# Two of four block transposes moved from TensorE to the DMA crossbar, beside the opening loads

## The chip, the cores and the metric

One core of one Trainium2 chip. The time is device microseconds of one execution; a kernel is run several times and the median is quoted. The kernel before takes 215.1 us (215.06 to 215.31 in its first three runs).

## The reference

A layer norm feeds a sliding, dilated local attention (32 heads of 20, 8 keys at distance 0, 2, ... 14) and a dense MLP with GELU; both are added to the input.

```python
S, D, F, H, W, dil = 2048, 640, 1536, 32, 8, 2
xn  = layernorm(x)                               # (2048, 640), bf16
qkv = xn @ wqkv                                  # 640 -> 1920
logits[h, s, w] = q[h, s] . k[h, s - 2*w] * 20**-0.5      # masked where s - 2*w < 0
att = softmax(logits) applied to v[h, s - 2*w]
out = x + att @ wo + gelu(xn @ w1 + b1) @ w2 + b2
```

## The kernel before

The 2048 rows are worked in four chunks of 512, a chunk in four blocks of 128 rows. Every matmul over D here takes the normalised rows transposed (`xnT`). In chunks 1 to 3 a DMA does that (`dma_start_transpose` from one SBUF tile to another, called a crossbar transpose below; one of a block with nothing beside it landed 2.4 us after its issue), issued from the SP queue from 20.5 us on, when the opening loads are nearly over. In chunk 0 TensorE does it, five 128x128 transposes a block into PSUM and a copy on ScalarE out of it, since the DMA engines are still busy with loads (94% from 6.5 to 25.3 us). The q, k and v projections of chunk 0 are made block by block, so that work can begin when the first block is there: 75 matmuls of 128x128 a block, in five groups.

A small planner in the kernel (class `Plan`) orders all pieces: each has an engine, an assumed length, needs, PSUM buffers and a rank; the emitted order per engine is then fixed.

```python
nc.sync.dma_start(x_sb[:, 0, :], x_nb[:, 0, :])
nc.scalar.dma_start(x_sb[:, 1, :], x_nb[:, 1, :])
for s in range(3):                                           # wq, wk, wv
    nc.sync.dma_start(wqkv[s][:], wqkv_v[:, :, s * D : (s + 1) * D])
    if s == 0:
        nc.sync.dma_start(x_sb[:, 2:BPC, :], x_nb[:, 2:BPC, :])
...
for n in range(1, NCH):                                      # chunks 1 to 3 of x
    cs = slice(n * BPC, (n + 1) * BPC)
    nc.sync.dma_start(x_sb[:, cs, :], x_nb[:, cs, :])
nc.sync.dma_start(w1_sb[:], ...)                             # first MLP weights
...
def do_tp(n, bl):                                            # chunk 0, TensorE
    tp = psA.tile([P, 2 * CH], BF16, tag="acc", name="tp")
    for t in range(KT):
        nc.tensor.transpose(tp[:, t * P : (t + 1) * P], xn[:, t * P : (t + 1) * P], ident[:])
def do_tc(n, bl):                                            # chunk 0, ScalarE
    nc.scalar.copy(xnT[:, :, bl * P : (bl + 1) * P], tp[:, 0 : KT * P]...)
def do_td(n, bl):                                            # chunks 1 to 3, crossbar
    nc.sync.dma_start_transpose(xnT[:, :, bl * P : (bl + 1) * P], tiles["xn", n, bl][:])
def do_gj(bl, g):                                            # one group of a block's projections
    ...
    for i, (which, to) in enumerate(slots):
        for ti in range(KT):
            nc.tensor.matmul(ps[:, i, :], lhsT=wqkv_p[which][:, ti, to, :],
                             rhs=tiles["xnT", 0][:, ti, cs], start=(ti == 0), stop=(ti == KT - 1))
```

Of the kernel before, what the change touches and what calls it, by code (L numbers as in the profile page):

```python
# [11 lines left out]
ALU = mybir.AluOpType  # L12
AX = mybir.AxisListType
BF16 = mybir.dt.bfloat16
F32 = mybir.dt.float32
PE, VE, SE, DQ = "pe", "ve", "se", "dq"


class Plan:
# [101 lines left out]
S, D, F, H, W, DIL = 2048, 640, 1536, 32, 8, 2  # L121
P = 128
# [3 lines left out]
CH = 512  # L126
# [7 lines left out]
LASTB = S // P - 1  # L134
# [4 lines left out]


RANK = {
    "ad02": 53.9, "ad11": 29.1, "av2": -13.3, "f11": 8.8, "f12": -3.3, "gc1": 31.2, "ge3": -70.6, "gj1": 9.7,
    "gj2": -47.4, "o01": 8.4, "o02": -60.5, "o10": 1.1, "o11": -5.1, "o23": -111.4, "oc1": 83, "pj11": -38.5,
    "pj21": -36.7, "qk3": -41.5, "st2": 58.4, "st3": 210.8, "xn1": 20.2, "xn2": 19.2,
}


def make_plan(fns, offsets=RANK):

    pl = Plan(offsets)  # L150
# [6 lines left out]
    def f(kind, *a):  # L157
        return lambda: fns[kind](*a)
# [6 lines left out]
    for n in range(NCH):  # L165
        base = n * PERIOD
        prev = base - PERIOD
        early = base + (-37.0 if n == 1 else -85.0)
        xnT, q, k, v, oT = (("xnT", n), ("q", n), ("k", n), ("v", n), ("oT", n))
# [11 lines left out]
        for bl in range(BPC):  # L181
            xn, tp = ("xn", n, bl), ("acc", "tp", n, bl)
            pl.add(f"xn{n}{bl}", SE if n else VE, 0.81 if n else 0.42, early + -4.0 if n else -99, [f"rc{n}" if n else f"rc{n}{bl}"], f("xn", n, bl), [xn])
            if n > 0:
                pl.add(f"tc{n}{bl}", DQ, 4.0 if n > 1 else 2.7, early - 3.0, [f"xn{n}{bl}"], f("td", n, bl), [xn, xnT], 21.5)
                continue
            pl.add(f"tp{n}{bl}", PE, 0.3, early + -3.0 if n else -99, [f"xn{n}{bl}"], f("tp", n, bl), [xn, tp])
            pl.add(f"tc{n}{bl}", SE, 0.65, early + -3.0 if n else -99, [f"tp{n}{bl}"], f("tc", n, bl), [tp, xnT])
# [5 lines left out]
        if n == 0:  # L194
            for bl in range(BPC):
                for g, parts in enumerate(GROUPS):
                    ps, last = ("acc", "g", bl, g), max(p[0] for p in parts)
# [57 lines left out]
        for bl in range(BPC):  # L255
            ob = ("osb", n, bl)
            O = [("O", n, bl)] if n < NCH - 1 or bl % 2 == 0 else [("acc", "lo", n, bl), ("acc", "hi", n, bl)]
            final = n * BPC + bl == LASTB
            last = None
            for pc in range(5):  # L260
                need = [last] if last else [f"ge{n}{ft}" for ft in range(FT)] + [f"xb{n}", "ld"]
                if pc == 4:
                    need.append(f"ot{n}")
                us = (0.65, 0.65, 0.65, 0.65, 1.08)[pc] if final else (0.82, 0.82, 0.82, 0.82, 1.37)[pc]
                last = pl.add(f"o{n}{bl}{pc}", PE, us, base + PERIOD + 8.0 + 8.0 * bl, need, f("o", n, bl, pc, ("lo",) if final else ("lo", "hi")), O + (hTs if pc == 0 else hTs[3 * pc : 3 * pc + 3] if pc < 4 else [oT]))
            if final:
                pl.add("xl", VE, 0.42, base - 40, ["ld"], f("xl"))
                pl.add("oclo", VE, 0.65, base, [last, "xl"], f("oclo"), O + [ob])
                last = pl.add("ohi", PE, 1.05, base + PERIOD + 90, [last], f("ohi"), O)
                pl.add("ochi", VE, 0.25, base, [last], f("ochi"), O + [ob])  # L270
                continue
            pl.add(f"oc{n}{bl}", SE, 0.78, base, [last], f("oc", n, bl), O + [ob])
            pl.add(f"od{n}{bl}", SE, 0.0, base, [f"oc{n}{bl}"], f("od", n, bl), [ob])
# [4 lines left out]
def kernel(  # L278
# [16 lines left out]
    nc = tc.nc  # L295
# [6 lines left out]
    consts = ctx.enter_context(tc.tile_pool(name="consts", bufs=1))  # L302
# [15 lines left out]
    x_sb = wts.tile([P, NCH * BPC, D], BF16, name="x_sb")  # L318
# [3 lines left out]
    wo2 = wts.tile([P, KT, D], BF16, name="wo2")  # L322
    b1_rt = consts.tile([P, P], BF16, name="b1_rt")
    b2bc = consts.tile([P, D], BF16, name="b2bc")
    xlast = consts.tile([P, D], BF16, name="xlast")
    wqkv_v = A_wqkv.rearrange("(t p) n -> p t n", p=P)
    b2_bcast = bass.AP(tensor=B_b2.tensor, offset=B_b2.offset, ap=[[0, P], [1, D]])
    nc.sync.dma_start(x_sb[:, 0, :], x_nb[:, 0, :])
# [48 lines left out]
    tiles = {}  # L377

    def get(key, make):
        if key not in tiles:  # L380
            tiles[key] = make()
        return tiles[key]
# [48 lines left out]
    def do_tc(n, bl):  # L431
# [3 lines left out]
            tiles["tp", n, bl][:, 0 : KT * P].rearrange("p (t m) -> p t m", t=KT),  # L435
        )

    def do_td(n, bl):
        xnT = get(("xnT", n), lambda: xtp.tile([P, KT, CH], BF16, tag="xnT", name="xnT"))
        nc.sync.dma_start_transpose(xnT[:, :, bl * P : (bl + 1) * P], tiles["xn", n, bl][:])  # L440
# [12 lines left out]
        nc.gpsimd.dma_start(dst, b2bc[:].unsqueeze(1).to_broadcast([P, cs.stop - cs.start, D]), accum_op=ALU.add)  # L453

    def do_xl():
        nc.vector.tensor_tensor(out=xlast[:], in0=x_sb[:, LASTB, :], in1=b2bc[:], op=ALU.add)


    def qkv_tile(n, which):
# [224 lines left out]
    last = (NCH - 1, BPC - 1)  # L684

    def do_oclo():
        osb = outp.tile([P, D], BF16, tag="osb", name="osb")
        tiles["osb", last] = osb
        nc.vector.tensor_tensor(out=osb[:, 0:CH], in0=tiles["lo", *last][:], in1=xlast[:, 0:CH], op=ALU.add)  # L689
        nc.sync.dma_start(out_sd[LASTB * P :, 0:CH], osb[:, 0:CH])  # L690

    def do_ohi():
# [3 lines left out]
    def do_ochi():  # L696
        osb = tiles["osb", last]
        nc.vector.tensor_tensor(  # L698
            out=osb[:, CH:D], in0=tiles["hi", *last][:, 0 : D - CH], in1=xlast[:, CH:D], op=ALU.add
        )  # L700
        nc.scalar.dma_start(out_sd[LASTB * P :, CH:D], osb[:, CH:D])

# [2 lines left out]
    with tc.manual_schedule(engines=engines):  # L705

        idle = psA.tile([P, CH], F32, tag="acc", name="idle")
        for _ in range(WARM):
            nc.tensor.matmul(idle[:, 0:P], lhsT=ident[:], rhs=ident[:], start=True, stop=True)
        for t in make_plan(fns).run():  # L710
            t["fn"]()
# [30 lines left out]
```

## Time and profile before

| stage of the profiled execution (span 212.9 us) | from, us | to, us |
|---|---|---|
| warm-up matmuls on the identity, first loads | 0 | 6.5 |
| projections of chunk 0 | 6.5 | 25.3 |
| MLP, attention, projections of chunks 1 to 3, output | 25.3 | 210.1 |
| last sum and store | 210.1 | 212.9 |

TensorE has hardly a pause between its first transpose and its last matmul, and the chain that ended last consists of it for 95%. So a change pays by what it takes off TensorE, or costs by the time that TensorE stands still. (The windows leave it 1.8 us idle.) The first MLP matmul starts at 25.32 us; from there to the end it is 187.6 us. I use these two numbers below as "the end of the projections" and "the rest". The lines are shown in the prediction.

### The profile page before, as it was taken

The numbers are of one execution on the slowest core, as the hardware profiler recorded it, in microseconds if no ns is written. First come the engines' busy times: TensorE is split into PE (matmuls) and PEld (weight loads), VectorE is DVE, ScalarE is ACT, GpSimd is POOL, SyncE is SP. The second block draws the span as 40 slices with busy tenths as digits, with TensorE's granted clock in tenths as the row PEclk, the third lists the DMA queues.
The fourth block names the chain that finished last, engine by engine and source line by source line (L and its number), as shares of the span: only waits on it lengthen the run. The fifth ranks groups of instructions, "written<-read, shape, count | busy, mean of one in ns | idle before, by whom it ended". The sixth has DMA issues, their size and how long they took to land.

```text
span 212.9 us, 3943 instructions
## 1 busy us (share of the span) xinstructions
PE 206.1 (97%) x1665; PEld 121.2 (57%) x1690; DVE 174.2 (82%) x176; ACT 106.8 (50%) x190; POOL 19.5 (9%) x36
## 2 busy tenths in 40 slices
PE   7899999999999999999999999999999999999994
PEld 7799844654544556556555555554555455555552
DVE  2849999459999999999999999999499789982001
ACT  3567899689565733635428273420297321351210
POOL 2000000000011015101001010110101011101220
PEclk9999999999999999999999999999999999999999
DMA  6999417973939579977002180211021822202223
GB/s 211 364 363 381 78 31 198 386 67 41 228 115 140 76 261 211 197 115 190 0 3 31 17 210 4 31 7 27 2 31 14 216 32 31 26 8 32 34 31 62
DMA packets 23433, 23.95 MB, mean 112 GB/s; under 512 B 9080, under 2 KB 20600, under 8 KB 23416
## 3 DMA queue, kind: packets, MB, share of 16 engines
q1 hardware_dynamic: 17832, 16.49, 28.0%
q0 software_dynamic: 4144, 4.92, 17.3%
q10 hardware_dynamic: 1440, 2.29, 3.7%
q8 instruction: 13, 0.21, 0.4%
q14 instruction: 4, 0.03, 0.0%
HBM read 10.00 MB, written 7.54 MB: 82 GB/s over the span
## 4 chain that ended last, share of the span: by engine, by line
PE 95%; DMA 1%; DVE 1%; issue 1%; ACT 0%
PE lo L668 26%; PE hps L637 24%; PE pps L472 23%; PE gps L489 8%; PE hi L670 8%; PE L L541 4%; DMA x_sb<-in_A_x_dram 1%; PE tp L429 0%; DVE stats L388 0%; DVE stats L389 0%; ACT xnT L433 0%; DVE xn L415 0%; DVE mv L390 0%; DVE osb L698 0%; PE b_tp L369 0%
## 5 line engine op out<-in xcount | busy, mean ns | idle before, releaser
L637 PE MATMUL hps<-xnT,w_sb 128*128 128x512 bf16 x236 | 53.9, 379 | 0.3 <-issue 0.2
L668 PE MATMUL lo<-w_sb,hT 128*128 128x512 bf16 x186 | 52.6, 379 | 0.0
L615 DVE TENSOR_TENSOR pv<-vT,ax 128x2560 bf16<-128x2560 bf16 x32 | 45.9, 1484 | 4.9 <-PE L L541 2.9
L522 DVE TENSOR_TENSOR prod<-qT,kT 128x2560 bf16<-128x2560 bf16 x32 | 45.5, 1484 | 0.0
L670 PE MATMUL hi<-w_sb,hT 128*128 128x128 bf16 x192 | 40.3, 219 | 0.3
L648 ACT ACTIVATE hT<-hps,b1T 128x512 bf16<-128x512 f32 x48 | 31.4, 687 | 17.0 <-PE hps L637 13.7
L637 PEld LDWEIGHTS <-w_sb 128*128 128x128 bf16 x240 | 22.8, 98 | 26.8 <-issue 0.4
L675 ACT CAST osb<-lo 128x512 bf16<-128x512 f32 x15 | 8.8, 585 | 50.9 <-PE hi L670 22.9
L624 DVE TENSOR_TENSOR pv<-pv 128x5120 bf16<-128x5120 bf16 x12 | 33.9, 2822 | 0.3
L668 PEld LDWEIGHTS <-hT 128*128 128x128 bf16 x192 | 18.7, 98 | 22.6 <-issue 0.2
L681 POOL DMA_DIRECT2D out_dram<-osb x15 | 12.9, 862 | 110.4 <-ACT osb L676 110.4
L668 PE MATMUL lo<-wo,oT 128*128 128x512 bf16 x74 | 22.1, 379 | 0.1
L670 PEld LDWEIGHTS <-hT 128*128 128x128 bf16 x192 | 18.4, 98 | 1.9
L670 PE MATMUL hi<-wo,oT 128*128 128x128 bf16 x80 | 16.9, 219 | 0.3
L472 PE MATMUL pps<-xnT,wk_sb 128*128 128x512 bf16 x71 | 16.9, 380 | 0.2
L472 PE MATMUL pps<-xnT,wq_sb 128*128 128x512 bf16 x72 | 16.9, 380 | 0.2
L472 PE MATMUL pps<-xnT,wv_sb 128*128 128x512 bf16 x73 | 16.9, 379 | 0.1
L689 DVE TENSOR_TENSOR osb<-lo,xlast 128x512 bf16<-128x512 f32 x1 | 0.7, 690 | 16.1 <-PE lo L668 16.1
L507 ACT CAST kT<-pps 128x512 bf16<-128x512 f32 x15 | 8.8, 584 | 8.8 <-PE pps L472 8.6
L668 PEld LDWEIGHTS <-oT 128*128 128x128 bf16 x80 | 7.8, 98 | 9.4
L472 PEld LDWEIGHTS <-wk_sb 128*128 128x128 bf16 x75 | 8.6, 118 | 7.5 <-issue 0.4
L472 PEld LDWEIGHTS <-wv_sb 128*128 128x128 bf16 x75 | 8.6, 117 | 7.2
(63 smaller groups left out, 208.2 us busy)
## 6 DMA issues: line engine op xcount, KB each, us to landing
w_sb<-in_B_w_dram SPq DMA_DIRECT2D x2, 1920.0 KB, 11.5
out_dram<-osb POOLq DMA_DIRECT2D x15, 160.0 KB, 3.4
ax<-attn SPq DMA_DIRECT2D x8, 256.0 KB, 5.1
ax<-attn ACTq DMA_DIRECT2D x8, 256.0 KB, 5.5
x_sb<-in_A_x_dram SPq DMA_DIRECT2D x3, 640.0 KB, 11.4
out_dram<-x_sb SPq DMA_DIRECT2D x3, 640.0 KB, 4.7
out_dram<-b2bc POOLq DMA_DIRECT2D x3, 640.0 KB, 7.7
wq_sb<-in_A_wqkv_dram SPq DMA_DIRECT2D x1, 800.0 KB, 4.9
```

The lines of the kernel that those rows point to most:

```text
L472: nc.tensor.matmul(ps[:], lhsT=wqkv_p[which][:, ti, to, :], rhs=xnT[:, ti, :], start=(ti == 0), stop=(ti == KT - 1),)
L489: nc.tensor.matmul(ps[:, i, :], lhsT=wqkv_p[which][:, ti, to, :], rhs=tiles["xnT", 0][:, ti, cs], start=(ti == 0), stop=(ti == KT - 1),)
L507: nc.scalar.copy(dest[:, to, off : off + CH], tiles["pps", n, which, to][:])
L522: nc.vector.tensor_tensor(out=prod[:, i, :, :], in0=qkv_tile(n, 0)[:], in1=qkv_tile(n, 1)[:, :, off : off + CH], op=ALU.mult,)
L615: nc.vector.tensor_tensor(out=pv[:, i, :, :].rearrange("p t (j c) -> p t j c", j=BPC), in0=qkv_tile(n, 2)[:, :, off : off + CH].rearrange( ...
L624: nc.vector.tensor_tensor(out=ta[:], in0=ta[:], in1=tb[:], op=ALU.add)
L637: nc.tensor.matmul(ps[:], lhsT=w1_sb[:, ti, ft * P : (ft + 1) * P], rhs=tiles["xnT", n][:, ti, :], start=(ti == 0), stop=(ti == KT - 1),)
L648: nc.scalar.activation(hT[:], tiles["hps", n, ft][:], ACT.Gelu_apprx_tanh, bias=b1T[:, ft : ft + 1], scale=1.0)
L668: nc.tensor.matmul(lo[:], lhsT=lhs, rhs=rhs[:, 0:CH], start=first, stop=last)
L670: nc.tensor.matmul(hi[:, 0 : D - CH], lhsT=lhs, rhs=rhs[:, CH:D], start=first, stop=last)
L675: nc.scalar.copy(osb[:, 0:CH], tiles["lo", n, bl][:])
L681: nc.gpsimd.dma_start(rows, tiles["osb", n, bl][:], accum_op=ALU.add)
```

## The change

Its intent: ten transposes less on TensorE and two copies less on ScalarE, by transposing blocks 2 and 3 of chunk 0 with the crossbar. The transposes are issued from the ScalarE queue, since the SP queue is filled with loads. The ranks of the planner were set anew for it. The bias add of the last rows now works in place, and its piece is placed anew in the plan. (The projections of chunk 0 block by block were there before the change.)

```diff
 RANK = {
-    "ad02": 53.9, "ad11": 29.1, "av2": -13.3, ... "gj1": 9.7, "gj2": -47.4, ...
+    "ad02": 35.4, "av1": -3.8, "av2": 86, ... "gj0": 23.6, "gj1": 4.1, "gj3": 6.8, ...
 }
...
+            if bl > 1:
+                pl.add(f"ts{n}{bl}", SE, 0.45, -99, [f"xn{n}{bl}"], f("ts", n, bl), [xn, xnT])
+                pl.add(f"tc{n}{bl}", DQ, 1.6, -99, [f"ts{n}{bl}"], lambda: None, [xn, xnT], slack=1.5)
+                continue
             pl.add(f"tp{n}{bl}", PE, 0.3, ...)
             pl.add(f"tc{n}{bl}", SE, 0.65, ...)
...
+    def do_ts(n, bl):
+        nc.scalar.dma_start_transpose(tiles["xnT", n][:, :, bl * P : (bl + 1) * P], tiles["xn", n, bl][:])
...
-        nc.vector.tensor_tensor(out=xlast[:], in0=x_sb[:, LASTB, :], in1=b2bc[:], op=ALU.add)
+        nc.vector.tensor_tensor(out=x_sb[:, LASTB, :], in0=x_sb[:, LASTB, :], in1=b2bc[:], op=ALU.add)
```

## The prediction

> **What bounds the kernel now.** I read the page's busy shares first, then the chain that ended last in order of time, then a table of windows by stage, and last the timeline and the DMA view of the first 30 us, where the change acts.
>
> ```profile
> PE 206.1 (97%) x1665; PEld 121.2 (57%) x1690; DVE 174.2 (82%) x176; ACT 106.8 (50%) x190; POOL 19.5 (9%) x36
> ...
> PE 95%; DMA 1%; DVE 1%; issue 1%; ACT 0%
> ```
>
> TensorE (PE) is busy for 206.1 us of the 212.9 us span, and the chain consists of PE for 95%. The vector engine (82%) has slack: near the end it idles 16.1 us waiting for PE. So a change pays only by taking work off PE's queue or closing one of its gaps. The window table (columns: stretch, its length, then busy us of PE, PEld, DVE, ACT, POOL, then clock, DMA share, GB/s):
>
> ```profile
> 0.00:6.50 6.50, 4.29 (x41) 4.12 (x42) 2.59 (x9) 2.08 (x4) 1.32 (x17) 1.00 0.74 238
> 6.50:25.30 18.80, 18.43 (x321) 18.10 (x322) 14.96 (x48) 13.45 (x34) 0.00 (x0) 1.00 0.94 313
> 25.30:210.10 184.80, 183.38 (x1308) 98.99 (x1330) 156.37 (x119) 91.30 (x153) 18.21 (x19) 1.00 0.44 88
> ```
>
> The 4.29 us before 6.5 are warm-up matmuls on the identity. PE's useful work begins at 6.47 (first transpose) and ends at 210.1. In the projections of the first chunk it is idle 18.80 - 18.43 = 0.37 us, in all the rest 184.80 - 183.38 = 1.42 us. That bounds every gain: even with no gap left, 1.8 us come off. And in that stretch the DMA engines are 94% busy, at 313 GB/s: the loads that the new transposes must share with. The chain there, start and length in us:
>
> ```profile
> 6.47 0.47 PE tp L429 x5
> ...
> 7.70 3.51 PE gps L489 x60
> 11.21 0.56 PE tp L429 x10
> 11.77 0.56 PE gps L489 x10
> 12.33 0.11 PE b_tp L369
> 12.44 0.04 issue
> 12.48 13.00 PE gps L489 x230
> ```
>
> From 7.70 on PE runs without a break. 230 projection matmuls take 13.00 us, 56.5 ns each; a block needs 75, hence 4.24 us. The ten transposes of blocks 2 and 3 take 0.56 us of the chain, though each matmul record is 219 ns long: they are pipelined.
>
> [...] the 160 KB block issued at 26.98 us with nothing beside it moved at up to 307 GB/s and landed 2.4 us after the start of issue. The kernel's later transposes are on another queue (SP); the first of those started only at 20.53[...]. [...] between 2.6 and 3.3 us, with one block of x from each queue and packets of about equal size, the shares were
>
> ```profile
> q1 hardware_dynamic: 112, 0.13, 53.5%
> q10 hardware_dynamic: 109, 0.13, 49.8%
> ```
>
> so a transpose on the ScalarE queue (q10) need not stand behind the megabytes queued on SP (q1), but must alternate with them.
>
> **The change part by part.**
>
> Removed from PE: 10 transposes, 0.56 us of the chain (above).
>
> Removed from ScalarE: two copies out of PSUM of 0.70 us, 1.40 us. Added there: two transpose issues. The records on SP are
>
> ```profile
> L440 SPq DMA_TRANSPOSE xnT<-xn x12: 1200/1217/3254, 20.5 to 74.0; - x12
> ```
>
> 1.20 us each[...]. An ordinary load cost ScalarE 0.42 us to issue and SP 0.40, so I take 1.20 for ScalarE too; the diff's planner has 0.45. ScalarE thus gains 2.40 - 1.40 = 1.0 us of blocked queue in a stretch where it is busy 13.45 of 18.80 us; evictions slip by one issue, which four PSUM buffers (groups of up to 1.1 us on PE) absorb.
>
> Transfer, block 2: the normalised block (xn) was written at 9.30 to 9.75 us. Issue about 9.85 to 11.05; in the lone case data began to move about 1.05 us after issue began, hence at 10.9. In this shape it is 672 packets, 42 per engine; alone they take about 0.6 us (160 KB at some 280 GB/s), 14 ns each. Between 11 and 14 us the loads moved 858 packets in 3 us, 17.9 per engine and us, 56 ns each. Strictly alternating, the block needs 42 x (56 + 14) = 2.9 us: moved by 13.8, landed about 0.5 us later, as alone: 14.3, an estimate from these rows. Block 3, issued about 11.6 to 12.8 after an eviction, follows on the same ring: moved by 16.7, landed 17.3.
>
> When PE needs it. PE's order is fixed by the planner; its new ranks make block 1 and block 2 urgent, then block 3, and block 0 filler. I took only the order from its rules, the times from the trace: q of blocks 0 and 1 from 7.70 (40 matmuls), k of block 1 (20), the fifth tiles of q and k (10), k of block 0 (20), v of block 1 (20), then block 2. That is 110 x 56.5 ns = 6.2 us after 7.70, so 13.9; allowing 0.15 us the other way, 13.75 to 13.9. All of block 2 follows before block 3: 14.3 + 4.24 + 0.28 = 18.8 at the earliest, after the 17.3 at which block 3 lands. So one stall: block 2, 14.3 - 13.8 = 0.5 us.
>
> Elsewhere: loads behind the pair come about 1.0 us later (320 KB at about 313 GB/s). The first MLP weights, issued at 8.81, landed 14.3 us later at 23.1; some 24.1 is still before their first use at about 25.3. The new ranks reshuffle later stages, but PE's work there is the same 183.4 us, with 1.42 us of gaps; I give the reshuffle 0 +/- 0.6 us. The last row's residual (add of bias in place instead of a tile of its own) is the same single 0.49 us add on DVE, off the path. Projections were already by single blocks; their count and shapes don't change.
>
> Sum: 215.1 - 0.56 + 0.5 + 0 = 215.0. As the alternation is the pessimistic reading[...], I lean 0.2 lower: 214.8.
>
> **The rivals.** (a) The transposes land by 13.7: the full 0.56 us comes off, and if the new order also closes half of the 1.42 us of gaps, 213.8. For: the lone transfer of 2.4 us would land at 12.3. Against: DMA engines 94% busy. (b) The wait replaces the work and is larger: the issue on ScalarE starts late behind an eviction,[...] three loads of x took 4.14 us to issue and one transpose 3.25. Then block 2 lands at 16 to 17.5, PE stalls 2 to 3.5 us less what it saves: 216.5 to 218. [...] (c) ScalarE's blocked queue becomes the bound: evictions late by 2.4 us, PE out of PSUM buffers. For: both issues may be placed back to back. Against: PE fills four buffers in about 4 us. Up to 1 us of stall, 215.6. (d) All of it is hidden, since PE can do other projections meanwhile: that is (a).
>
> **Range and chances.** The gain is bounded: 0.56 + 1.8 = 2.4 us is 1.1%, so faster by over 2% (below 210.8) would need less matmul work: 1%. Slower by over 2% needs 4.3 us net, a landing of block 2 after about 18.6 us, with PE in order behind it: 4%. Within 2%: 95%. The range 213.8 to 216.3 holds (a), (c), my sum and the mild end of (b).
>
> **What would show it.** In the changed profile: no transposes of PE after the first ten, 20 x 219 ns records become 10; two DMA transposes on the ACT queue from about 9.85 and 11.6 us, 1.2 us each; landing 4 to 5 and 5 to 6 us after issue; one PE gap of about 0.5 us near 13.8 us, in a projection group of block 2 that waits for a DMA on xnT; the end of the projections within 0.5 us of 25.3. I am wrong if that gap exceeds 2 us, if PE waits for ScalarE's evictions or the MLP weights instead, if the issues take 0.45 us, or if the gaps after 25.3 us change by more than 0.6 us.

No term of the sum is among the cuts: it is still 215.1 - 0.56 + 0.5 + 0 = 215.0. The 0.2 taken off to reach 214.8 is a guess of mine that no trace supports.

## The result, and the profile after

The changed kernel takes 223.82 us (median of 6, from 222.12 to 225.19), before 215.12 us (median of 6 in the same rounds). The ratio is 1.0393, with a 95% interval of 1.0337 to 1.0449: slower by 3.9%. A ratio is the mean time of one kernel's fast runs over that of the other's fast runs of the same rounds, so it isn't quite the ratio of the medians.

The page of the changed kernel, busy shares and chain by engine:

```profile
PE 209.0 (95%) x1680; PEld 122.2 (56%) x1680; DVE 173.9 (79%) x176; ACT 108.1 (49%) x190; POOL 19.5 (9%) x36
...
PE 90%; DMA 5%; DVE 1%; ACTq 1%; ACT 1%; issue 0%
```

TensorE has ten transposes less to do, yet is busy 2.9 us longer (the two don't compare: 25 matmul records that were missing before are there now), and the DMA's share of the chain has grown from 1% to 5%. The window table for the projections of chunk 0, columns as in the prediction:

```profile
6.50:25.30 18.80, 14.06 (x217) 13.63 (x214) 8.90 (x30) 7.62 (x19) 0.00 (x0) 0.91 0.93 309
```

Before, TensorE was busy 18.43 of these 18.80 us and did 321 instructions; now it is busy 14.06 and does 217, and the granted clock is 0.91 instead of 1.00. The chain of that stretch:

```profile
7.56 2.09 PE gps L495 x35
9.65 8.59 DMA xnT<-xn
18.23 0.05 issue
18.28 11.03 PE gps L495 x165
29.32 0.11 PE b_tp L372
29.43 1.52 PE gps L495 x25
```

Where before 300 projection matmuls followed each other, the chain now runs through one transfer of 8.59 us, the crossbar transpose of block 2. The instructions concerned in order of time; the bracket tells how long the engine had been idle, and on what:

```profile
9.65 1.33 ACTq L442 DMA_TRANSPOSE xnT<-xn  x1
...
11.10 1.23 ACTq L442 DMA_TRANSPOSE xnT<-xn  x1
...
18.28 1.80 PE L495 MATMUL gps<-xnT,wq_sb 128*128 128x128 bf16 x20 [4.42 <-DMA xnT<-xn]
```

TensorE has done all that its fixed order puts before block 2 at 13.86 us and waits for 4.42 us. All transposes from the ScalarE queue together, issue to landing (two of them, so the extremes are block 2 and block 3):

```profile
DMA to landing us min/median/max: 8.6/10.6/12.5
```

After the wait the matmuls are slow. Two windows of one microsecond, columns as above (the number of matmuls started stands behind the first busy time, the granted clock third from the end):

```profile
20.00:21.00 1.00, 1.00 (x12) 1.00 (x11) 0.00 (x0) 0.59 (x1) 0.00 (x0) 0.50 1.09 412
24.00:25.00 1.00, 1.00 (x22) 1.00 (x20) 0.14 (x1) 0.95 (x4) 0.00 (x0) 1.00 0.00 0
```

The clock was at half from 18.93 to 22.35 us, 3.41 us. "Busy" says nothing of this: both windows read 1.00, with 12 matmuls in one and 22 in the other. The 165 matmuls from 18.28 on took 11.03 us; at 56.5 ns they would have taken 9.32, so the half clock cost 1.71 us.

Where the 6.7 us of the span (212.9 to 219.6) came from, in the profiled executions:

| part | us |
|---|---|
| projections begin at 7.56 instead of 7.70 | -0.14 |
| ten transposes not on the chain | -0.56 |
| wait for block 2 | +4.42 |
| half clock after the wait | +1.71 |
| sum; the first MLP matmul starts at 30.78 instead of 25.32, +5.46 | +5.43 |
| the rest, 188.8 instead of 187.6 us | +1.23 |

The profiled execution is the fastest of the six; the median lost 2 us more. The executions of the changed kernel differ by 3 us, those of before by 0.3 to 1. The mean clock tells why in part: 0.992 in the fastest (half clock for about 2 x 0.008 x 219.6 = 3.5 us), 0.977 in one of 224.21 us (2 x 0.023 x 221.8 = 10 us). So half clock of one to three times 3.4 us fits the six, and 1.71 us is the least that it cost.

Why did the transfer take 8.6 us? The DMA queues in two stretches (packets, MB, busy share of 16 engines; q1 is SP's queue with the loads, q10 ScalarE's with the transposes), first between 15 and 17 us with the rows of x as the loads, then between 18 and 22 us with the MLP weights:

```profile
q1 hardware_dynamic: 439, 0.56, 77.6%
q10 hardware_dynamic: 446, 0.11, 26.1%
```

```profile
q1 hardware_dynamic: 475, 1.45, 91.8%
q10 hardware_dynamic: 476, 0.12, 13.5%
```

The queues advance by equal numbers of packets, 439 to 446 and 475 to 476, not by equal bytes. A packet of the transpose is 256 B, one of x 1280 B, one of the MLP weights 3072 B: of the bytes the transpose gets a sixth in the first stretch and a thirteenth in the second. But turn-taking began late. The first packet of block 2 moved at 13.9 us, 4.2 us after its issue began; between 9.6 and 13.8 us q10 moved nothing at all.

### The profile page after: what moved, and what is told of

The parts are those of the page before. It is cut to its first block, busy times and chain, and to the rows that moved or that the text cites. A ratio compares the mean times of both kernels' runs of the same rounds, so it can differ in the third digit from the quotient of the medians.

```text
span 219.6 us, 3958 instructions
## 1 busy us (share of the span) xinstructions
PE 209.0 (95%) x1680; PEld 122.2 (56%) x1680; DVE 173.9 (79%) x176; ACT 108.1 (49%) x190; POOL 19.5 (9%) x36
## 4 chain that ended last, share of the span: by engine, by line
PE 90%; DMA 5%; DVE 1%; ACTq 1%; ACT 1%; issue 0%
PE lo L674 27%; PE hps L643 24%; PE pps L478 21%; PE hi L676 7%; PE gps L495 7%; PE L L547 4%; DMA xnT<-xn 4%; DMA x_sb<-in_A_x_dram 1%; ACTq L605 1%; DVE stats L391 0%; DVE stats L392 0%; ACT xnT L436 0%; ACT qT L513 0%; PE tp L432 0%; DVE xn L418 0%
## 5 line engine op out<-in xcount | busy, mean ns | idle before, releaser
L674 PE MATMUL lo<-w_sb,hT 128*128 128x512 bf16 x192 | 53.6, 379 | 0.0
L654 ACT ACTIVATE hT<-hps,b1T 128x512 bf16<-128x512 f32 x48 | 31.1, 688 | 22.0 <-PE hps L643 18.2
L643 PEld LDWEIGHTS <-w_sb 128*128 128x128 bf16 x240 | 23.0, 98 | 27.2 <-issue 0.5
L674 PEld LDWEIGHTS <-hT 128*128 128x128 bf16 x192 | 18.7, 98 | 22.8 <-issue 0.8
L674 PE MATMUL lo<-wo,oT 128*128 128x512 bf16 x80 | 23.1, 379 | 0.0
L478 PE MATMUL pps<-xnT,wq_sb 128*128 128x512 bf16 x75 | 17.2, 379 | 0.6 <-ACT qT L513 0.6
L478 PE MATMUL pps<-xnT,wv_sb 128*128 128x512 bf16 x75 | 17.2, 379 | 0.0
L478 PE MATMUL pps<-xnT,wk_sb 128*128 128x512 bf16 x75 | 16.8, 379 | 0.0
L695 DVE TENSOR_TENSOR osb<-lo,x_sb 128x512 bf16<-128x512 f32 x1 | 0.7, 692 | 16.1 <-PE lo L674 16.1
L478 PEld LDWEIGHTS <-wq_sb 128*128 128x128 bf16 x75 | 8.6, 118 | 7.9 <-issue 0.9
L513 ACT CAST qT<-pps 128x512 bf16<-128x512 f32 x15 | 8.5, 583 | 8.6 <-PE pps L478 8.6
```

Of the source, the lines that this page charges most:

```text
L478: nc.tensor.matmul(ps[:], lhsT=wqkv_p[which][:, ti, to, :], rhs=xnT[:, ti, :], start=(ti == 0), stop=(ti == KT - 1),)
L643: nc.tensor.matmul(ps[:], lhsT=w1_sb[:, ti, ft * P : (ft + 1) * P], rhs=tiles["xnT", n][:, ti, :], start=(ti == 0), stop=(ti == KT - 1),)
L654: nc.scalar.activation(hT[:], tiles["hps", n, ft][:], ACT.Gelu_apprx_tanh, bias=b1T[:, ft : ft + 1], scale=1.0)
L674: nc.tensor.matmul(lo[:], lhsT=lhs, rhs=rhs[:, 0:CH], start=first, stop=last)
```

## The experiments

All kernels gave correct results. "End of projections" is the start of the first MLP matmul, "the rest" the time from there to the end of the span; landings are read from the trace of the profiled execution.

| kernel | us (median) | ratio to before | block 2, 3 landed | end of projections | the rest |
|---|---|---|---|---|---|
| before | 215.1 | 1 | on TensorE | 25.3 | 187.6 |
| changed | 223.8 | 1.039 | 18.2, 23.6 | 30.8 | 188.8 |
| rank_only | 217.6 | 1.011 | on TensorE | 25.2 | 189.8 |
| dma_only | 239.0 | 1.109 | 19.3, 24.7 | 32.7 | 203.6 |
| same_order_act | 223.2 | 1.038 | 18.6, 23.9 | 32.6 | 188.2 |
| warm_fill | 226.0 | 1.048 | 18.7, 25.3 | 33.4 | 190.5 |
| b2_last | 222.7 | 1.034 | 19.5, 26.4 | 30.6 | 190.2 |
| w1_first | 223.5 (one) | - | 19.3, 22.2 | 32.1 | 188.8 |
| act_gated | 219.2 | 1.018 | 16.4, 21.4 | 28.6 | 189.0 |
| sp_first | 218.2 | 1.014 | 13.5, 14.2 | 27.2 | 188.8 |
| same_order_sp | 217.5 | 1.011 | 13.2, 16.8 | 26.9 | 187.9 |
| replan | 238.8 | 1.108 | 13.5, 14.9 | 25.4 | 211.2 |
| one_late | 215.8 | 1.001 | -, 21.4 | 25.8 | 188.0 |

The theory after reading the two traces: the loads that stand ahead of the transposes, and then beside them, delay their landing; TensorE waits; the wait halves its clock. The rivals: the new ranks make a worse order (R1); ScalarE's queue, blocked by two issues, is the cause (R2); the half clock has another cause than the wait (R3).

### The ranks alone, and the transposes alone

**rank_only**: the kernel before with the new table of ranks.

```diff
 RANK = {
-    (ranks of before)
+    (ranks of the changed kernel)
```

> The kernel before with only the new ranks (blocks 2 and 3 still transposed on TensorE). My theory (the late crossbar transposes make the stall): within 1.5 us of before, 214.5 to 216.5, no gap of TensorE over 0.7 us before 26 us. Rival (the new order of work itself costs the time): over 219 us, with the gaps of TensorE after 31 us as in the changed kernel.

217.56 us, ratio 1.0108 (1.0091 to 1.0126). Neither range was met: 1 us above mine, well below the rival's. TensorE has no gap over 0.5 us before the MLP; the projections end at 25.2 us. The loss lies in the rest, +2.2 us, most of it in two gaps near 120 and 128 us. The waits of TensorE between 110 and 130 us:

```profile
PE pps L472 <- ACT vT L507: 1.3, 1, 1.3
...
PE hps L637 <- ACT hT L648: 0.7, 1, 0.7
```

So the new ranks do cost something in this setting, about 1%: TensorE waits there for ScalarE to clear PSUM. In the changed kernel those two gaps don't appear; it has one of 0.57 us at 97.6.

**dma_only**: the changed kernel with the ranks of before.

```diff
 RANK = {
-    (ranks of the changed kernel)
+    (ranks of before)
```

> The changed kernel with the ranks of before put back; the crossbar transposes stay. My theory: the stall stays, since block 2 is again wanted near 13.9 us and lands near 18: 221 to 225 us, a gap of TensorE of 3.5 to 5 us at 13.9, then a stretch at half clock. Rival (the order of work costs it): 214 to 217 us.

238.97 us: far above both. The wait is there, as the theory says (4.80 us at 14.7, then 6.8 us of half clock; the projections end at 32.7). But the rest takes 203.6 us, 16 more than in before, with ten gaps, most of them for PSUM evictions on ScalarE, and two more spells of half clock. So either these ranks can't go with crossbar transposes, or the planner, which had a different list of pieces to place, made a poor order out of ranks set for another list. That had to be told apart.

**same_order_act**: the order of before is kept on every engine. Only the pieces change: nothing is emitted for the transposes and copies of blocks 2 and 3, and the two crossbar transposes are issued where the changed kernel has them.

```diff
     def do_tp(n, bl):
+        if bl > 1:
+            return
...
     def do_tc(n, bl):
+        if bl > 1:
+            return
...
     def do_gc(bl, g):
+        if (bl, g) in ((1, 0), (0, 1)):
+            by_dma(nc.scalar, 3 if g else 2)      # crossbar transpose of block 3 or 2
```

> The kernel before with its instruction order kept on every engine, except that the ten TensorE transposes and two ScalarE copies of blocks 2 and 3 are gone and two crossbar transposes on the ScalarE queue, in the places they have in the changed kernel, stand for them. In this order block 2 is wanted near 13.3 us and block 3 near 17.5 us (13.6 and 17.8 in before, less the transposes). My theory (the time lies in the landings, 18.2 to 19.5 and 23.6 to 26 us, not in the ranks): a gap of about 5 us, half clock for 3.4 to 7 us, projections end 5 to 8 us later than in before, 220 to 224 us, of which at most 1.5 us come after the projections. Rival (the very slow 239 us with the ranks of before shows that those ranks can't be used with crossbar transposes): over 230 us.

223.20 us, ratio 1.0378 (1.0340 to 1.0416), the time of the changed kernel. The chain of the profiled execution:

```profile
9.63 8.94 DMA xnT<-xn
18.57 0.05 issue
18.62 14.15 PE gps L496 x210
```

A wait of 5.56 us, half clock for 6.8 us, projections end 7.3 us late, and the rest is within 0.6 us of before. With the ranks of before, the order of before and nothing but the transposes changed, the whole loss is there. R1 falls as the cause of the 4%. The 239 us of dma_only were the planner's new order, not the transposes.

### What delays the landing

**sp_first**: the two transposes go to the SP queue ahead of the loads of chunks 1 to 3 and of the first MLP weights, which are issued after them.

```diff
-    for n in range(1, NCH): nc.sync.dma_start(x_sb[...])      # at the start
-    nc.sync.dma_start(w1_sb[:], ...)
...
     def do_ts(n, bl):
-        nc.scalar.dma_start_transpose(...)
+        nc.sync.dma_start_transpose(...)
+        if bl == 3:
+            later_loads()                                     # the loads removed above
```

> The changed kernel with the two transposes issued on the SP queue ahead of the loads of chunks 1 to 3 and of the first MLP weights, which are issued after them. My theory (the loads queued ahead delay the transposes): block 2 lands by 13.5 and block 3 by 14.5 us, the gap at 13.9 us is under 0.3 us, no half clock, 214 to 216 us; the first MLP weights land about 1 us later than in before. Rival (a crossbar transpose is slow by itself beside any load, or the gap comes from ScalarE's blocked queue or from the order): the gap stays over 2 us and the time over 218 us.

Issue to landing of the two:

```profile
DMA to landing us min/median/max: 2.8/3.2/3.6
```

3.6 and 2.8 us instead of 8.6 and 12.5, landed at 13.5 and 14.2: the wait for the transposes is gone and the clock stays at 1.0 in the profiled execution (one of the other three has 0.99). The time is 218.17 us, missing my 214 to 216; of the rival, the time is there (over 218) but not the gap of over 2 us. Two new waits took part of the place, 1.22 us at 20.8 and 0.80 us at 25.0: ScalarE, in whose order the normalised rows of chunk 1 come before those evictions, stood before the statistics of chunk 1, whose rows now landed at 17.3 instead of 13.7 us, and so did not clear PSUM for TensorE. And the first MLP weights landed at 27.13 instead of 23.07 us (I had expected 1 us later), just before the first MLP matmul at 27.20: without those two waits the MLP could not have begun earlier either. The rest is that of the changed kernel (188.8).

**act_gated**: as in the changed kernel on the ScalarE queue, but the later loads are held back on SP until block 3 is normalised.

```diff
     def do_ts(n, bl):
         nc.scalar.dma_start_transpose(...)
+        if bl == 3:
+            nc.vector.tensor_copy(x_sb[:, BPC, 0:1], tiles["xn", n, bl][:, 0:1])   # the load waits for this
+            later_loads()
```

> The changed kernel, transposes on the ScalarE queue as in it, but the loads of chunks 1 to 3 and of the first MLP weights are held back on SP until block 3 is normalised (about 10.5 us), so that only the v weights are queued ahead. My theory (the transposes wait for what the loads have already handed to the DMA engines): the transposes begin to move by 12 us, both have landed by 14.5 us, no gap of TensorE near 13.9 us over 0.7 us and no half clock; time as with the transposes ahead of the loads on SP, 216.5 to 219.5 us, since the late loads of chunk 1 hold back ScalarE's evictions as there. Rival (it is the ScalarE queue, not the loads ahead: its issue or its ring is slow): landing of block 2 after 16 us, time over 220 us.

A partial miss. Block 2 was issued at 11.15 us (in this execution the first loads of q and x landed 1.4 us later than in before) and its first packet moved at 12.45, 1.3 us later: with little ahead, the ScalarE queue starts some 3 us sooner after its issue than in the changed kernel. R2 falls as far as the queue itself goes. Issue to landing, block 2 and block 3, and the first matmuls of block 2:

```profile
DMA to landing us min/median/max: 5.2/7.0/8.8
```

```profile
16.41 1.31 PE L499 MATMUL gps<-xnT,wq_sb 128*128 128x128 bf16 x20 [1.60 <-DMA xnT<-xn]
```

But both landings were later than I said, 16.4 and 21.4. The data packets of block 2 had all moved by 13.2 us. What came late, at 15.0 to 15.8, were the 32 packets of 4 B that follow the data of each block, and by then the held-back loads, released at 11.96, filled the engines. Block 3, issued at 12.61 and so behind these loads, moved its first packet at 17.2. Holding loads back until the transpose *could* be issued isn't enough. TensorE waited 1.60 us, without half clock in the profiled execution (one of the other three has a mean clock of 0.992). Here too the MLP weights landed late, at 28.52 us, just before their first matmul at 28.57. 219.19 us, with an interval of the ratio from 1.0113 to 1.0238, so whether this is 2% slower than before is unclear.

**w1_first**: the MLP weights before chunks 1 to 3 of x, to see by what measure the loads stand ahead.

```diff
+    nc.sync.dma_start(w1_sb[:], ...)
     for n in range(1, NCH): nc.sync.dma_start(x_sb[...])
-    nc.sync.dma_start(w1_sb[:], ...)
```

> The changed kernel with the first MLP weights loaded before, not after, chunks 1 to 3 of x. Their packets are 3072 B and take 130 ns per engine, those of x 1280 B and 56 ns. In the changed kernel block 2 began to move 3.2 us later than it could (13.9 against 10.7), while each engine did some 59 packets of loads. Theory A, a fixed number of packets stands ahead: 26 of v weights, then 33 of 3072 B: start near 16.4 us. Theory B, a fixed amount of bytes or of time stands ahead: start near 13.9 again. Theory C, a turn is not a packet: whenever it starts, the transfer keeps 3.5 us; by single packets in turn it takes 42 x 0.14 = 5.9 us. Under A with single packets block 2 lands near 22.5 us and the time is over 226 us.

The first packet moved at 13.8, as in the changed kernel, so theory A falls: each engine did only 27 packets of loads between 10.7 us and then (58 in the changed kernel), but 76 KB (72 KB there). B remains. Bytes or time, the runs can't tell apart, because the loads moved at the same rate in all: in all seven kernels whose SP queue was full, a transpose on the ScalarE queue began to move 4.0 to 4.3 us after its issue began, and 95 to 97 KB of loads per engine went first. From 14 to 17 us the two queues moved 350 and 356 packets, so equal numbers again, with packets of 3072 B. The transfer itself took 4.7 us (first packet until as many data packets as block 2 has), between the 5.9 that I had expected for turns by packets and the 3.5 of theory C. The same measure is 3.4 to 4.1 us in the five other kernels with both blocks and a full queue, so the size of this one execution doesn't rule C out by itself; the equal numbers are what speaks against it. To landing it was 5.5 us:

```profile
9.82 9.48 DMA xnT<-xn
19.30 0.05 issue
19.35 11.31 PE gps L495 x165
```

Block 2 landed later than in the changed kernel, block 3 earlier (22.2 against 23.6), as its companions were now the small packets. Because block 2 came earlier than my A said, so did the end: 223.46 us, one execution.

### What the wait does to TensorE

**warm_fill**: 76 dummy matmuls in front of block 2, so that TensorE works through the wait.

```diff
     def do_gj(bl, g):
+        if bl == 2 and g == 0:
+            fill = psO.tile([P, CH], F32, tag="lo", name="fill")
+            for _ in range(76):
+                nc.tensor.matmul(fill[:, 0:P], lhsT=ident[:], rhs=ident[:], start=True, stop=True)
```

> The changed kernel with 76 dummy 128x128 matmuls on TensorE (about 4.3 us) between the last group before block 2 and the first of block 2, so TensorE works through the wait. If the half clock after the gap is a cost of the idle time: clock 1.0 throughout, the 45 slow matmuls of 90 ns become 57 ns, 1.5 to 2 us faster than the changed kernel, 220 to 223 us. If it comes from something else (the load of the chip at that moment): the half clock stays, and so does the time, 222 to 225 us.

Neither: 225.97 us, slower than the changed kernel. The wait for block 2 shrank to 0.80 us and its matmuls ran at full clock: with the wait mostly filled, the half clock at this place is gone, so R3 falls there. But TensorE then came to block 3 before it landed:

```profile
11.18 14.11 DMA xnT<-xn
25.28 0.14 issue
25.42 6.54 PE gps L499 x85
```

It waited 1.99 us, and the clock halved after this wait instead, from 26.1 to 29.5 us. In the changed kernel the wait for block 2 and the half clock had hidden the wait for block 3, which landed at 23.6 while TensorE came to it at 24.4. Block 3 landed later here (25.3); the dummy matmuls use no DMA, and I have no reason for it but the spread between executions.

**b2_last**: all groups of blocks 0 and 1 before block 2.

```diff
-    "gj3": 6.8, ...
+    "gj2": 30.0, "gj3": 31.0, ...
```

> The changed kernel with ranks that put every group of blocks 0 and 1 before block 2, then block 3. TensorE then has work until about 16.1 us instead of 13.9. My theory (what counts is when the blocks land, 18.2 and 23.6 us, and work of block 0 was put after the wait instead of into it): one gap of about 2 us at 16, one of about 1 us before block 3, projections end near 28 instead of 31 us, 218 to 221 us. Rival (a gap of 2 us also halves the clock): projections end near 29.5, 220.5 to 222.5 us.

222.71 us, just above the rival's range. TensorE worked until 16.56, as expected, waited 2.96 us for block 2, ran 3.4 us at half clock, waited 0.88 us for block 3, and then did block 3:

```profile
11.58 14.78 DMA xnT<-xn
26.36 0.05 issue
26.41 4.38 PE gps L495 x75
```

Here it is plain why no order of these pieces helps: 75 matmuls remain after block 3 has landed, 4.2 us at 56.5 ns each. Landing at 23.6 to 26.4 us, block 3 by itself keeps the projections from ending before 27.9 to 30.6 us; in the kernel before they end at 25.3. The rest shows the same two gaps as rank_only, 5.4 us later.

### Is there a version that gains?

**one_late**: block 2 back on TensorE, block 3 alone by the crossbar and last in order, with the ranks of before.

```diff
-            if bl > 1:
+            if bl > 2:
...
-    (ranks of the changed kernel)
+    (ranks of before, and "gj3": 20.0)
```

> The ranks of before, with block 2 transposed on TensorE again and only block 3 by the crossbar from the ScalarE queue, its groups put last, after blocks 0, 2 and 1. TensorE then needs block 3 only at about 7.6 + 0.3 + 225 x 0.0565 = 20.6 us. My theory: issued about 10.5, it moves 4.2 us later at 14.7 and lands near 18.5 to 19.5, so no gap, no half clock: before less 0.28 us, 214.5 to 215.5 us. Rival (any crossbar transpose beside these loads costs TensorE time, for example through ScalarE's 1.2 us issue or through weights that land later): over 216.5 us.

215.79 us beside 215.33, ratio 1.0009 (0.9985 to 1.0032): the same. The block took 10.4 us from issue to landing, 21.4 us, later than I said but just before TensorE came to it. TensorE did not wait for it, and the clock stayed at 1.0. Nor was there a gain: the projections end at 25.8 us, against 25.3 in before. TensorE waited 0.46 us at 12.5 for ScalarE to clear PSUM, an eviction that stood behind the 1.33 us of the transpose's issue (10.96 to 12.29), and 0.18 us for the bias row; that is more than the 0.28 us of five transposes.

**same_order_sp**: the order of before, transposes on SP ahead of most loads: block 2, chunk 1 of x, block 3, the other loads.

```diff
     def do_xn(n, bl):
...
+        if bl == 2: by_dma(nc.sync, 2); load_x(1)
+        if bl == 3: by_dma(nc.sync, 3); load_x(2); load_x(3); (first MLP weights)
```

> The same, with the transposes on the SP queue ahead of loads: block 2, then chunk 1 of x, then block 3, then chunks 2 and 3 and the first MLP weights. Block 2 is issued about 9.9 and lands about 13.4; chunk 1 of x (1.75 us of transfer) lands about 15.5, block 3 about 16, the MLP weights about 1.2 us later than in before (24.3). My theory: no half clock, gaps under 0.5 us up to 25 us, 214.4 to 215.6 us, so at best the 0.56 us of the ten transposes are won, 0.26%. Rival (anything put ahead of the loads costs as much as it saves): 216 us or more, with a gap for evictions behind the statistics of chunk 1, or for the MLP weights.

217.53 us, ratio 1.0111 (1.0092 to 1.0129): the rival's range. The blocks landed in time (13.2 and 16.8), but TensorE waited 1.05 us at 11.8 for the bias row, which was queued behind the v weights and had not landed, and 0.42 us at 26.5 for the first MLP weights, which landed at 26.9 instead of 23.1. 320 KB more at some 313 GB/s explain 1.0 us of those 3.8; a stretch in which the DMA engines moved little, below, is part of the rest. The window from 11 to 14 us in before, then in this kernel (DMA share and GB/s are the last two):

```profile
11.00:14.00 3.00, 2.96 (x53) 2.90 (x51) 0.47 (x2) 2.32 (x6) 0.00 (x0) 1.00 1.07 363
```

```profile
11.00:14.00 3.00, 1.95 (x34) 1.77 (x33) 0.17 (x1) 0.99 (x3) 0.00 (x0) 1.00 1.00 88
```

88 GB/s instead of 363: while the transpose of block 2 stood between loads in one queue, the engines moved 0.26 MB in 3 us. From 11.3 us on, some 19 packets of the transpose, about one per engine, took 1.1 to 1.2 us each, where a packet of x takes 0.06. The changed kernel has a hole of the same kind: from 14.45 us on, 17 packets of both queues took 0.56 to 0.75 us each, and from 14.6 to 15.1 us the engines moved some 20 GB/s. Before has no such packet of these two queues between 8 and 20 us. In the seven kernels with a full SP queue this hole begins 0.5 to 0.7 us after the transpose's first packet. I have not found what the engines wait for there.

**replan**: as sp_first, with the ranks of before, the loads in the order chunk 1, MLP weights, chunks 2 and 3, and the planner told when they land.

```diff
-        for n in (1, 2, 3): load x;  load w1
+        load x chunk 1; load w1; load x chunks 2, 3
...
-            land = ... 11.4 + 1.9 * n
+            land = ... (0, 17.2, 22.6, 24.4)[n]
```

> Both transposes on the SP queue ahead of the later loads, the ranks of before, and what the late loads hold back put right: chunk 1 of x is loaded next, then the first MLP weights, then chunks 2 and 3, and the planner is told when they land (17.2, 22.6, 24.4 us), so that ScalarE does not wait for the statistics in front of evictions. My theory: transposes land by 13.5 and 14.2 us, no gap over 0.7 us before 26 us; 214.3 to 216 us, at best 0.5 us faster than before. Rival (the DMA engines are full until 23 us, so what is put ahead of the loads costs as much as it saves, or the moved statistics delay VectorE and what follows): 216.5 to 220 us with gaps of TensorE after 26 us.

In the stage that it was made for it did what I said: landed at 13.5 and 14.9, projections end at 25.4, the single gap 0.70 us at 9.9 for k weights that landed late. But the planner made a new order for everything after it, with a gap of 8.9 us at 63.6, two more of 3.0 and 3.5 us, and 17 us of half clock after them: 238.76 us. Like dma_only it says nothing against the transposes, and much about re-running a planner that was tuned for one list of pieces.

## Why the prediction was wrong

**What held.** The step "When PE needs it" was right: 13.75 to 13.9 us, measured 13.86. So were the issue ("1.20 for ScalarE too": 1.33 and 1.23, not the planner's 0.45), the 0.56 us, that ScalarE's blocked queue would be absorbed (no TensorE gap for an eviction in this stage of the changed kernel; in the orders of dma_only and one_late there is one, of 0.55 and 0.46 us), the equal turns of the queues (446 packets against 439, 476 against 475), and the bound on any gain. The transposes of the two queues did not overlap: the first one on SP started after the last one on the ScalarE queue had landed (27.16 after 23.62 us in the changed kernel, 21.70 after 21.41 in one_late).

**Two readings were off** without changing the outcome. "In all the rest 184.80 - 183.38 = 1.42 us" of idle TensorE, half of which rival (a) hoped to win, are places of missing records, as said above. The lone transpose began to move 1.18 us after its issue began, not 1.05. (Its rate, up to 307 GB/s, is below that of the loads, 363 GB/s between 11 and 14 us.)

**The step that failed** is "Transfer, block 2 ... hence at 10.9 ... moved by 13.8, landed about 0.5 us later, as alone: 14.3". It landed at 18.23. Two terms of it were mis-sized. The start: I took some 1 us from the lone transpose, where nothing stood ahead; beside a full SP queue it was 4.2 us, so the first packet moved 3.0 us later than I said. The prediction said that the transpose "need not stand behind the megabytes queued on SP". It need not stand behind all of them, but 95 KB of loads per engine, or 4.2 us, went between its issue and its first packet; act_gated (1.3 us with little ahead) shows that they delay it, and the seven kernels with 4.0 to 4.3 us. The transfer itself: 2.9 us predicted, about 3.4 until as many data packets as the block has had moved (13.9 to 17.3), with the hole of 0.5 us in it; and 0.9 us from there to landing, not 0.5. For block 3 I took the 56 ns packets of x for its companions; they were the MLP weights at 3072 B by then, and it landed at 23.62 instead of 17.3.

**The step "So one stall: block 2, 14.3 - 13.8 = 0.5 us"** follows from the same number; it was 4.42 us.

**A term that was missing** is the clock. I counted a wait as its own length. The trace of before, at a mean clock of 1.000, has no half clock in its span, so nothing in it gave a price. The runs do: in the changed kernel the half clock came after the gap of 4.42 us, lasted 3.41 us and cost 1.71 us; in dma_only and same_order_act it lasted 6.8 us after gaps of 4.80 and 5.56 us. Rival (b), "PE stalls 2 to 3.5 us", lacks this term.

**The step "I give the reshuffle 0 +/- 0.6 us"** was off by size: +1.23 us in the changed kernel (0.57 of it the gap at 97.6 us for an eviction on ScalarE, 0.35 after the last matmul), +2.2 us in rank_only. With the order of before kept, the rest is +0.4 to +0.6 us (same_order_sp, same_order_act).

**The rivals.** Rival (b) named the right outcome, a wait in place of the work, with 216.5 to 218 us, but by other causes (a late issue on ScalarE, or a long one like the 4.14 us for three loads and the 3.25 us for a transpose on SP); the issues were prompt, 1.33 and 1.23 us. I gave 4% to a landing "after about 18.6 us" as the case for slower by over 2%. It landed at 18.2, a wait that comes to 3.9 us net (4.42 - 0.56); the half clock (1.71) and the rest (1.23) did the remainder. The low weight came from one reading: the share of the two queues between 2.6 and 3.3 us, 112 packets to 109, taken when both were empty at the start. It showed how the engines divided their time once both queues were moving packets, not how long a newcomer waits to get there: 4.2 us in the changed kernel.

## What to carry to other kernels

In these runs a transfer from a second queue had two delays beside a stream of loads: the time until its first packet moved (4.0 to 4.3 us), and its share, which went by packets (446 of 256 B to 439 of 1280 B), not by bytes; measure both in the trace at the moment concerned, not from a lone transfer. Before moving work off the bottleneck engine, compare what it takes there (0.56 us here) with the slack of what replaces it (a landing 8.6 us after issue against a need 4.2 us after it), and consider the clock after a wait (1.7 us lost here in 3.41 us at half rate): it was halved after the 1.99 us in warm_fill, though not after a wait of 2.64 us in dma_only (last section). When a list scheduler fixes the order, test a change in the old order first: crossbar transposes on the ScalarE queue took 223 us in the old order and 239 us re-planned.

Still open: whether the late start is a matter of bytes or of time, and what the hole in the DMA engines' work beside a transpose is.

## What was measured of transposes, turns and the clock

- A 160 KB transpose beside loads on the other queue landed 8.6 to 9.5 us after issue as the first of two (10.4 in one_late, as the only one), against 2.4 alone, and in same_order_sp the loads around it fell from 363 to 88 GB/s for 3 us.
- In the changed kernel the two queues move equal numbers of records, 446 of 256 B against 439 of 1280 B, and 476 against 475 of 3072 B, which fits turns of one record or of equally many from each; the records don't tell which. The time until the newcomer's first packet was 4.0 to 4.3 us beside a full queue, and 1.3 us with little ahead (act_gated).
- The clock was halved after waits of TensorE of 4.42 us (changed kernel), 4.80 (dma_only), 5.56 (same_order_act), 2.96 (b2_last) and 1.99 (warm_fill), for 3.4 us in the changed kernel, b2_last and warm_fill and 6.8 us in the other two. It was not halved after waits of 2.64 us (dma_only, at 173.7 us), 1.60 (act_gated) and 0.80 (warm_fill). So the length of the wait does not decide alone, and what else does was not shown.
